# Sums turned on VectorE in 32x32 blocks, nine buffers for P, and last chunks tile by tile

## The chip, the cores and the metric

The kernel runs on one core of a Trainium2 chip. The metric is the time of one execution on the device in microseconds (us), the median of several runs. The engines are TensorE (PE; its weight loads are listed apart as PEld), VectorE (DVE), ScalarE (ACT), GpSimd (POOL) and SyncE (SP). DMAs are issued by SP and, at a few places, by ACT; an instruction that issues one occupies its engine's queue for as long as the issue takes, and everything behind it there waits.

## The reference

The program computes attention and two feed-forward layers behind it, all in float32 (weights of the first layer arrive as 64-bit floats):

```python
q_rot, k_rot = rotate(q), rotate(k)                    # 4 batches, 8 heads, 576 positions, 64 wide
scores = matmul(q_rot, k_rot.T) / 8
attn = exp(scores - max(scores))
attn = attn / (sum(attn) + 1e-9)
x = matmul(attn, v)                                    # -> 2304 tokens x 512
h = maximum(x @ w_in, 0);  x2 = (h * h) @ w_out        # 512 -> 2048 -> 512
h = x2 @ w_in2;  g = maximum(h, 0) + alpha * minimum(h, 0)
out = g @ w_out2                                       # 512 -> 2048 -> 512
```

## The kernel before, in words

**Attention** (function `attention`, from line 66) works on 16 pairs of heads: 4 batches by 4 pairs of neighbouring heads (`n` counts them, 0 to 15). For one pair the steps are: K and Q are rotated on GpSimd (`rope`), turned by TensorE (`turn`) and split into a high and a low part; scores are computed by query tile `i` (0 to 4, the fifth of 64 rows for both heads, called **S4**) and head `j` (`scores`, L257, three products per half for the split parts); VectorE takes the row maximum (`top`, L262, tile `nm`); ScalarE takes the exponential with its row sum (`exps`, L271), the sum into one of the columns of `sums`; TensorE turns P (`trans`, L279, `trans_tail`, `trans_end`); the results are copied out of PSUM (`leave`, tiles `pt`, `ptt`); TensorE multiplies with V (`pv`, L341) in two halves of 288 columns into a bank `acc`; and `store` copies each half to a tile `st` (L177 on ACT, L179 on DVE) and, with the second one, sends the tile to `x` in DRAM (L351).

P is not divided before it meets V. Instead the reciprocals of the sums travel apart: `over` (**OD**, L317 and L318) adds 1e-9 and takes the reciprocal on VectorE; `over_turn` (**O**, L322) turns the 128x32 tile of sums by a TensorE product with the identity; `over_leave` (**OR**) copies nine rows to a tile `ri` on ScalarE (L328) and stores them to a DRAM array `r` with three DMAs (L331 twice, L332). The queue for x and r is SP, for the last two pairs ACT.

**The order** of attention is written out by a plan. `PLAN` gives each step of a pair a due time within a repeating period, and the engine that takes a copy where there is a choice ("A" or "V"). All steps of all pairs lie in one heap and are recorded by due time, pair `n` at n periods plus the step's time, so each engine works on parts of three pairs at once. The due times set an order only; nothing waits for a clock. `NP_` is the number of buffers of a P tile; `acc` (`NAC`) and `st` have one buffer each.

**The first feed-forward layer** (function `moe`) works on 6 blocks of 384 tokens. For a block it loads x and r in four chunks of 128 columns: `load_x` (L764, L766, tile `xt`, two buffers) issues one DMA of x and two of r, broadcast over 64 rows each; `join_x` (L772, on GpSimd for these) multiplies them, and `high_x` and `low_x` split the product. Chunks of the first blocks are prepared while attention still runs: `AHEAD_X` steps from 13.5 pairs on, and the steps of `FOLLOW_AT` within the last pair's time, each call `follow`, which takes the next piece of the layer's start: chunk loads, joins, weight loads (L501, tile `w64`), the weights' conversion on VectorE and ScalarE (`convert` L510, L511; `mask` L516; `grow` L520; `sign` L525, L526; `join` L531, L532), and the first units of products (L803 to L805: 12 products of 384 columns make one unit). These products stand among attention's own in TensorE's order, so they fill TensorE between the last pairs' steps. Behind the last pair the layer runs alone.

**The second layer** has three groups of two blocks and forms its first product by seven block products. Its second product (L822) adds up 16 chunks of the hidden width, chunk after chunk, into three accumulators, one for each tile of 128 tokens; when chunk 15 is through, `finish` copies the accumulators out (L860 on ACT, L862 on DVE) and `store` sends the rows to `out` by SP (L834), in one or two DMAs per tile.

Of the kernel before, what the change touches and what calls it, by code (L numbers as in the profile page):

```python
# [23 lines left out]
P = 128  # L24
# [10 lines left out]
NP_, NTB, NAC = 8, 3, 1  # L35
PTB = 2
RB = 1
PERIOD = 14.053
PLAN = {
# [26 lines left out]
def attention(tc, q, k, v, ident_d, rope_d, xd, rd, follow):  # L66
# [10 lines left out]
    with ExitStack() as at:  # L77
# [237 lines left out]
        def over(n):  # L315
            t = sums[n][:, 0:9]
            V.tensor_scalar(t, t, 1e-9, None, ALU.add)  # L317
            V.reciprocal(t, t)  # L318

        def over_turn(n):  # L320
            u = turned[n, "o"] = bank()
            T.transpose(u[0:32, 0:P], sums[n], ident)  # L322
# [696 lines left out]
```

## Time and profile before

| | us |
|---|---|
| median of 3 runs | 1055.24 (1054.94 to 1055.89) |
| the profiled execution, whole | 1058.53 |
| its span, first to last instruction | 1056.7 |
| TensorE busy in it | 1040.0 |
| VectorE busy | 712.2 |
| ScalarE busy | 585.1 |
| GpSimd busy | 375.6 |

The profile shows one execution. Its own time is some 3.3 us above the median of the runs, so a sum made from its rows is a difference, to be set against its own time and carried over to the median. Times within it count from the span's start. Attention takes the first 280 us, the two layers the rest. A row such as "S4 ... [0.28 <-ACT p L271]" says that the engine sat idle for 0.28 us before this instruction, and that what it waited for last was ScalarE's instruction on tile `p` of line 271. Idle time of an engine that is not the bottleneck costs nothing by itself; here TensorE is busy nearly all the time, so the few places where it is idle are the ones to look at. "PEclk" is the clock that TensorE was granted, as a share of full speed.

### The profile page before, as it was taken

To read this page: it belongs to the slowest core of one execution; us is meant where nothing else is said; L and a number is where in the kernel's file an instruction comes from. 1 tells how busy PE (TensorE), PEld (TensorE's weight loads), DVE (VectorE), ACT (ScalarE), POOL (GpSimd) and SP (SyncE) were. 2 spreads that over 40 slices of the span, in tenths; PEclk is the share of its full clock that TensorE was granted. 3 is DMA by queue.
4 is the path that set the end of the run, shared out by engine and by line. 5 is a ranking of instruction groups with operands and counts; after the bars stand their busy time and mean duration, and the time that the engine had idled before them with its cause. 6 is when DMAs were issued, how large, how long until landed. Compare 5 with 4: busy or idle time off the path is not lost.

```text
span 1056.7 us, 20163 instructions
## 1 busy us (share of the span) xinstructions
PE 1040.0 (98%) x7512; PEld 925.2 (88%) x7512; DVE 712.2 (67%) x1263; ACT 585.1 (55%) x1281; POOL 375.6 (36%) x365
## 2 busy tenths in 40 slices
PE   9999999999999999999999999999999999999997
PEld 5777777776799999999999999999889998899886
DVE  5888878887699896897887876655354462644521
ACT  4788888886588454645546455344243442444321
POOL 6867566753000001423324133255212660146200
PEclk9999999999999999999999999999999999999999
DMA  7033223155254334556566557998015750177011
GB/s 192 2 92 92 68 83 91 47 157 165 86 160 138 120 97 137 191 189 232 182 209 221 175 192 279 327 307 253 8 60 185 254 181 14 47 235 250 25 30 30
DMA packets 101137, 153.23 MB, mean 145 GB/s; under 512 B 16944, under 2 KB 61360, under 8 KB 101040
## 3 DMA queue, kind: packets, MB, share of 16 engines
q1 hardware_dynamic: 100152, 150.81, 45.1%
q8 instruction: 59, 0.97, 0.4%
q10 hardware_dynamic: 888, 1.14, 0.3%
q14 instruction: 38, 0.31, 0.1%
HBM read 114.61 MB, written 37.30 MB: 144 GB/s over the span
## 4 chain that ended last, share of the span: by engine, by line
PE 89%; DVE 4%; DMA 3%; ACT 1%; POOL 1%; issue 1%; SPq 1%; ACTq 0%; POOLq 0%; DVEq 0%
PE py L822 26%; PE ph L714 17%; PE ph L822 9%; PE acc L341 6%; PE ph L803 6%; PE ph L804 6%; PE ph L805 6%; PE sc L257 6%; PE ps L279 4%; DMA xt<-r 2%; PE ps L198 1%; DVE nm L262 1%; DVE gl L755 1%; DMA w<-x 1%; ACT p L271 1%
## 5 line engine op out<-in xcount | busy, mean ns | idle before, releaser
L755 DVE TENSOR_TENSOR gl<-g,gh 128x384 fp32r<-128x384 f32 x189 | 130.5, 693 | 120.3 <-PE py L822 104.2
L748 ACT ACTIVATE gh<-g 128x384 fp32r<-128x384 f32 x189 | 98.1, 521 | 146.7 <-PE py L822 142.1
L714 PE MATMUL ph<-T,xs 128*128 128x384 f32 x1008 | 176.4, 335 | 0.0
L714 PEld LDWEIGHTS ph<-T,xs 128*128 128x128 f32 x1008 | 175.3, 188 | 0.8 <-ACT w L706 0.4
L822 PE MATMUL py<-gh,w 128*128 128x384 f32 x560 | 146.2, 335 | 0.0
L262 DVE TENSOR_REDUCE nm<-sc 128x1 f32<-128x576 f32 x144 | 107.5, 755 | 38.2 <-PE sc L257 36.8
L803 PE MATMUL ph<-xs,held 128*128 128x384 f32 x368 | 123.7, 336 | 0.0
L805 PE MATMUL ph<-xs,held 128*128 128x384 f32 x368 | 123.5, 336 | 0.0
L804 PE MATMUL ph<-xs,held 128*128 128x384 f32 x368 | 123.4, 335 | 0.0
L271 ACT ACTIVATE p<-sc,nm 128x576 f32<-128x576 f32 x144 | 105.8, 736 | 23.5 <-DVE nm L262 23.2
L257 PE MATMUL sc<-nat 64*128 64x288 f32 x768 | 113.4, 307 | 1.0 <-ACT p L271 0.5
L822 PE MATMUL py<-w,gh 128*128 128x512 f32 x336 | 103.5, 389 | 0.0
L822 PEld LDWEIGHTS py<-gh,w 128*128 128x128 f32 x560 | 101.9, 188 | 0.0
L257 PEld LDWEIGHTS sc<-nat 64*128 64x128 f32 x768 | 98.8, 187 | 2.8 <-ACT p L271 1.9
L822 PE MATMUL py<-gl,w 128*128 128x384 f32 x280 | 94.1, 336 | 2.3 <-DVE gl L755 2.3
L772 POOL TENSOR_TENSOR xt<-xt 128x384 f32<-128x384 f32 x24 | 26.5, 1108 | 192.4 <-DMA xt<-x 172.2
L702 POOL TENSOR_TENSOR g<-g,m 128x384 f32<-128x384 f32 x62 | 67.1, 1089 | 72.3 <-ACT g L701 72.3
L279 PE MATMUL ps<-ident,p 64*128 64x64 f32 x1152 | 87.4, 226 | 1.8 <-ACT pt L177 1.7
L279 PEld LDWEIGHTS ps<-ident,p 64*128 64x128 f32 x1152 | 78.1, 139 | 9.9 <-issue 7.4
L341 PE MATMUL acc<-pt,vraw 128*64 128x288 f32 x512 | 79.8, 423 | 1.7 <-ACT pt L177 1.3
L822 PEld LDWEIGHTS py<-w,gh 128*128 128x128 f32 x336 | 63.0, 188 | 13.0
L803 PEld LDWEIGHTS ph<-xs,held 128*128 128x128 f32 x368 | 69.4, 188 | 0.6 <-issue 0.4
(161 smaller groups left out, 2132.4 us busy)
## 6 DMA issues: line engine op xcount, KB each, us to landing
xs<-ws SPq DMA_DIRECT2D x168, 256.0 KB
w<-in_moe_w_in_dram SPq DMA_DIRECT2D x32, 512.0 KB
w<-in_moe_w_out_dram SPq DMA_DIRECT2D x32, 512.0 KB
ws<-w SPq DMA_DIRECT2D x40, 256.0 KB
wk<-xs SPq DMA_DIRECT2D x16, 512.0 KB
w<-wk SPq DMA_DIRECT2D x14, 512.0 KB
xt<-x SPq DMA_DIRECT2D x24, 192.0 KB
xt<-r SPq DMA_DIRECT2D x48, 96.0 KB
```

The lines of the kernel that those rows point to most:

```text
L257: T.matmul(t[:, x, 0:SH], lhsT=lhs, rhs=k[b][h, c0:c0 + SH], start=y == 0, stop=y == 2)
L262: V.tensor_reduce(out=nm[n, i, j], in_=sc[n, i, j][:, :, 0:SH], axis=AX.XY, op=ALU.max, negate=True)
L271: A.activation(out=Pt[n, i][:, j * S:(j + 1) * S].rearrange("p (a b) -> p a b", a=2), in_=sc.pop((n, i, j))[:, :, 0:SH], func=AF.Exp, bias ...
L279: T.transpose(u[:, 64 * k:64 * k + 64], Pt[n, i][halves[h], c0:c0 + P], ident[halves[h], halves[h]])
L341: T.matmul(acc[n, hf][64 * j:64 * j + 64, 0:SH], lhsT=v2[:, j, c], rhs=t, start=c == 0, stop=c == 4)
L714: T.matmul(bank[c], lhsT=w[:, y0, ws_], rhs=t[:, y1], start=first_ and kc == 0 and n == 0, stop=kc == 1 and n == 2, skip_group_check=not f ...
L748: A.activation(out=hi, in_=hidden(layer, b, i), func=AF.Copy)
L755: V.tensor_tensor(out=lo, in0=hidden(layer, b, i), in1=gsp[u][0].bitcast(F32), op=ALU.subtract)
L803: T.matmul(ph[:, :W], lhsT=wh[:, cs], rhs=xh, start=(c == 0), stop=False)
L804: T.matmul(ph[:, :W], lhsT=wh[:, cs], rhs=xl, start=False, stop=False)
L805: T.matmul(ph[:, :W], lhsT=wl[:, cs], rhs=xh, start=False, stop=(c == KC - 1))
L822: T.matmul(acc, lhsT=x, rhs=y, start=(s0 and k == 0), stop=(s1 and k == 2))
```

## The change

Four things change.

1. The turn of the sums goes from TensorE to VectorE. `over` calls a VectorE transpose, which turns each 32x32 block of the 128x32 tile by itself; the result `rows` has, in each group of 32 partitions, nine rows of 32 positions. `over_turn` and `over_leave` with their steps O and OR are gone. `store` sends the reciprocals, directly behind x and on the same queue, with five DMAs: four of eight rows by 32 positions (one for each group of 32 partitions), and one for the tail.
2. `PLAN` and `FOLLOW_AT` have new numbers (the period goes from 14.053 to 14.054; the last step is at 37.08, before at 40.01), and some copies change engine.
3. P has nine buffers instead of eight.
4. In the last block of the second layer, chunks 13 and 14 are held back until chunk 15; then each of the three accumulators takes its products of the three chunks in turn. The second DMA of the last tile goes out by ACT's queue.

```diff
-NP_, NTB, NAC = 8, 3, 1
+NP_, NTB, NAC = 9, 3, 1
...
-    "PV14": (38.512, ""), "O": (39.246, ""), "ST1": (39.257, "A"), "OR": (40.006, ""),
+    "PV14": (36.220, ""), "ST1": (37.084, "V"),
...
             V.reciprocal(t, t)
-
-        def over_turn(n):
-            u = turned[n, "o"] = bank()
-            T.transpose(u[0:32, 0:P], sums[n], ident)
-            yield
-
-        def over_leave(n):
-            b, hp = pairs[n]
-            r = sm.tile([9, P], F32, name="ri")
-            A.activation(out=r, in_=turned.pop((n, "o"))[0:9, 0:P], func=AF.Copy)
-            eng = nc.scalar if n + 2 >= pairs_n else nc.sync
-            for j in range(2):
-                eng.dma_start(out=rd[hp, j, b * S:b * S + 512].rearrange("(i p) -> i p", i=4), in_=r[4 * j:4 * j + 4, :])
-            eng.dma_start(out=rd[hp:hp + 1, :, b * S + 512:b * S + 576], in_=r[8:9, :].rearrange("o (j c) -> o j c", j=2))
+            rows[n] = sm.tile([P, 32], F32, name="rows", bufs=2)
+            V.transpose(rows[n], sums[n])
...
-                (nc.scalar if n + 2 >= pairs_n else nc.sync).dma_start(out=xd[:, hp, b * S:(b + 1) * S], in_=sts.pop(n))
+                eng = nc.scalar if n + 2 >= pairs_n else nc.sync
+                eng.dma_start(out=xd[:, hp, b * S:(b + 1) * S], in_=sts.pop(n))
+                r, t = rd[hp, :, b * S:(b + 1) * S], rows.pop(n)
+                for g in range(4):
+                    eng.dma_start(out=r[:, 0:512].rearrange("j (i g p) -> g j i p", i=4, g=4)[g], in_=t[32 * g:32 * g + 8])
+                eng.dma_start(out=r[:, 512:576].rearrange("j (c p) -> j c p", c=2), in_=t[8:P:32])
...
+            held_back.append((i, wh, wl, gh, gl))
+            if (layer, b) == (1, NB - 1) and FC - LAST <= i < FC - 1:
+                return
             for e, acc in enumerate(accs[layer, b]):
                 es = slice(e * P, (e + 1) * P)
+                for x, wh, wl, gh, gl in held_back:
...
+            held_back.clear()
...
-                nc.sync.dma_start(out=rows, in_=y[c - t * P:c - t * P + w, :])
+                (nc.scalar if t == NTT - 1 and c > t * P else nc.sync).dma_start(out=rows, in_=y[c - t * P:c - t * P + w, :])
```

How instructions stand is shown at three places. First TensorE in the steady attention, around the six products of S4 of one pair (`qt` holds the two heads' last query rows); before:

```order
L198 MATMUL ps_3044<-ident_79,rotq_2705 128x64 x2
L341 MATMUL acc_3005<-pt_2553,vraw1_120 64x288 x2
L341 MATMUL acc_3005<-ptt_2552,vraw1_120 64x288 x2
L322 MATMUL ps_3072<-ident_79,sums_135 32x128
L257 MATMUL sc_3076<-nat_2758,qt1_130 128x288 x6
L341 MATMUL acc_3098<-pt_2842,vraw0_117 64x288 x2
```

and the same place after:

```order
L222 MATMUL ps_2766<-ident_79,rotk_2246 128x64
L257 MATMUL sc_2749<-nat_2463 128x288
L329 MATMUL acc_2770<-pt_2540,vraw1_120 64x288 x4
L257 MATMUL sc_2778<-nat_2463,qt0_129 128x288 x6
L329 MATMUL acc_2770<-pt_2540,vraw1_120 64x288 x2
L279 MATMUL ps_2793<-ident_79,p_2632 128x64
```

The turn of the sums (L322) is gone from its place ahead of S4, and the products with V that end an `acc` no longer stand there.

Second SP's queue from the store of pair 12 to that of pair 13, with chunk loads (`xt`) in between; before:

```order
L351 DMA x1_63<-st_4454 128x576
L331 DMA r1_64<-ri_4583 4x128 x2
L332 DMA r1_64<-ri_4583 2x1x64
L764 DMA xt_4188<-x1_63 128x384
L766 DMA xt_4188<-r1_64 64x384 x2
L764 DMA xt_4188<-x1_63 128x384
L766 DMA xt_4188<-r1_64 64x384 x4
L764 DMA xt_4188<-x1_63 128x384
L766 DMA xt_4188<-r1_64 64x384 x2
L764 DMA xt_4188<-x1_63 128x384
L766 DMA xt_4188<-r1_64 64x384 x4
L351 DMA x1_63<-st_4753 128x576
```

and after, from the end of pair 12's store on:

```order
L343 DMA r1_64<-rows_4358 2x4x32 x4
L344 DMA r1_64<-rows_4358 2x2x32
L758 DMA xt_4167<-x1_63 128x384
L760 DMA xt_4167<-r1_64 64x384 x2
L758 DMA xt_4167<-x1_63 128x384
L760 DMA xt_4167<-r1_64 64x384 x2
L758 DMA xt_4167<-x1_63 128x384
L760 DMA xt_4167<-r1_64 64x384 x3
L758 DMA xt_4167<-x1_63 128x384
L760 DMA xt_4167<-r1_64 64x384 x3
L758 DMA xt_4167<-x1_63 128x384
L760 DMA xt_4167<-r1_64 64x384 x4
```

Behind the last row pair 13's x follows, as before (L340, `x1_63<-st_4684`). Ten chunk loads and the stores of pairs 10, 11 and 12 stand from the first chunk load to that store in both orders; each store has five DMAs of r instead of three.

Third TensorE where the first unit of the layer (`ph`, L803 to L805 before, L797 to L799 after) meets pair 14's products with V (`acc`, the first half and then the second); before:

```order
L805 MATMUL ph_4976<-xs_4180,held0_4864 128x384
L279 MATMUL ps_4971<-ident_79,p_4597 128x64 x2
L341 MATMUL acc_4852<-pt_4634,vraw1_120 64x288 x2
L341 MATMUL acc_4852<-ptt_4633,vraw1_120 64x288 x2
L279 MATMUL ps_4971<-ident_79,p_4597 128x64
L279 MATMUL ps_5005<-ident_79,p_4801 128x64 x8
L279 MATMUL ps_5017<-ident_79,p_4597 128x64 x4
L279 MATMUL ps_5024<-ident_79,p_4832 128x64 x8
L341 MATMUL acc_5034<-pt_4634,vraw1_120 64x288 x2
L803 MATMUL ph_5039<-xs_4180,held0_4864 128x384
```

and after:

```order
L329 MATMUL acc_4830<-pt_4628,vraw1_120 64x288 x2
L329 MATMUL acc_4830<-ptt_4627,vraw1_120 64x288 x2
L279 MATMUL ps_4925<-ident_79,p_4783 128x64 x8
L309 MATMUL ps_4937<-ident_79,p_4616 128x64
L279 MATMUL ps_4941<-ident_79,p_4649 128x64 x8
L329 MATMUL acc_4951<-pt_4628,vraw1_120 64x288 x4
L797 MATMUL ph_4960<-xs_4159,held0_4862 128x384
```

Before, one whole unit lies ahead of the end of the first half's `acc`, and the second unit behind the first products of the second half. After, no unit lies ahead of the second half's first products; three units lie among the attention work behind them (before, two), and then comes the layer's run without attention. On VectorE the copy of the first half to `st` stands ahead of the last step of the first weight block in the new order, behind it in the old one; on ScalarE the store of pair 14 (x and five DMAs of r) stands ahead of one copy of `pt` and of `grow` of the third weight block, and VectorE's further steps on that block and the converts of the next two stand ahead of the copy that frees `acc` for the last half.

## Rows read from the trace of the kernel before

**Rows 1.** The page: busy us, share of the span, instructions.

```profile
PE 1040.0 (98%) x7512; PEld 925.2 (88%) x7512; DVE 712.2 (67%) x1263; ACT 585.1 (55%) x1281; POOL 375.6 (36%) x365
```

**Rows 2.** Busy us of PE, PEld, DVE, ACT, POOL by stretch; clock, DMA.

```profile
110.00:150.00 40.00, 39.67 (x519) 28.42 (x515) 33.03 (x65) 33.70 (x87) 28.46 (x24) 1.00 0.26 76
249.00:270.00 21.00, 18.65 (x155) 13.47 (x157) 14.79 (x29) 9.38 (x20) 3.44 (x4) 0.92 0.48 157
281.00:320.00 39.00, 39.00 (x227) 39.00 (x226) 31.70 (x58) 33.12 (x63) 0.00 (x0) 1.00 0.43 130
```

**Rows 3.** The chain of waits, next pair's S4: start, us, what.

```profile
115.52 1.06 PE sc L257 x6
```

**Rows 4.** Timeline around S4: start, us, engine, line, operation, [idle <-releaser].

```profile
100.33 0.28 PE L322 MATMUL ps<-ident,sums 128*32 128x128 f32 x1
...
100.45 0.20 ACT L271 ACTIVATION_READ_ACCUMULATOR p<-sc,nm 128x1 f32 x1
...
100.70 0.82 PEld L257 LDWEIGHTS sc<-nat,qt 128*128 128x128 f32 x6 [0.28 <-ACT p L271]
```

**Rows 5.** Groups by line and shape: busy us, mean ns, idle before.

```profile
L318 DVE RECIPROCAL sums<-sums 128x9 f32<-128x9 f32 x16 | 3.4, 215 | 0.5
```

**Rows 6.** SP's queue: the first chunk load and pair 13's x.

```profile
215.98 0.35 SPq L764 DMA_DIRECT2D xt<-x  x1
...
255.73 0.53 SPq L351 DMA_DIRECT2D x<-st  x1
```

**Rows 7.** Issues of the old r stores: ns minimum, median, maximum.

```profile
L331 SPq DMA_DIRECT2D r<-ri x28: 247/282/327, 57.0 to 256.7; - x28
...
L332 SPq DMA_DIRECT2D r<-ri x14: 595/616/676, 57.6 to 257.0; - x14
```

**Rows 8.** The chain of waits in the drain: start, us, what.

```profile
243.94 3.81 DMA xt<-r
...
248.93 2.13 DMA xt<-r
...
261.20 1.35 PE acc L341 x8
...
270.74 0.38 PE ph L803
...
273.03 0.64 PE ps L279 x8
273.67 1.12 PE acc L341 x8
...
277.81 2.65 PE acc L341 x20
```

**Rows 9.** Timeline of the drain, TensorE and VectorE.

```profile
256.32 1.08 PE L279 MATMUL ps<-ident,p 64*128 64x64 f32 x17 [1.19 <-ACT pt L177]
...
262.63 0.46 DVE L179 COPY st<-acc 128x288 f32<-128x288 f32 x1 [3.47 <-PE acc L341]
...
280.43 0.42 PE L803 MATMUL ph<-xs,held 128*128 128x384 f32 x1
```

**Rows 10.** Timeline of the drain, ScalarE and VectorE.

```profile
269.81 0.35 ACTq L351 DMA_DIRECT2D x<-st  x1
...
273.71 0.60 ACT L177 ACTIVATE pt<-ps 128x512 f32<-128x512 f32 x1 [0.79 <-PE ps L279]
274.20 0.76 ACT L520 ACTIVATE w<-w,pbias 128x512 uint32<-128x512 uint32 x1
...
275.29 0.69 DVE L525 SCALAR_TENSOR_TENSOR w<-w 128x512 uint32<-128x512 uint32 x1
276.02 0.43 DVE L526 TENSOR_SCALAR w<-w 128x512 uint32<-128x512 uint32 x1
```

**Rows 11.** Timeline of the end: SP's issues, the last copy.

```profile
1050.37 3.68 SPq L834 DMA_DIRECT2D out_dram<-g  x6
...
1051.11 0.60 ACT L860 ACTIVATE g<-py 128x512 f32<-128x512 f32 x1 [0.76 <-PE py L822]
```

More of the change, by code (lines that the diff above doesn't have):

```diff
@@ L34 @@
 PAIRS = 16
-NP_, NTB, NAC = 8, 3, 1
+NP_, NTB, NAC = 9, 3, 1
 PTB = 2
 RB = 1
-PERIOD = 14.053
+PERIOD = 14.054
 PLAN = {
[16 rows of a table removed]
[16 rows of a table added]
 }
@@ L58 @@
 X_AT, X_EVERY = 13.5, .12
-FOLLOW_AT = (0, 12.38, 12.91, 14.33, 14.34, 15.59, 15.63, 17.51, 17.52, 17.68, 17.69, 19.61, 20.89, 20.9, 21.23, 24.16, 24.17, 25.21, 26.43, 26.44, 28.94, 29.68, 29.69, 31.73, 33.66, 39.87)
+FOLLOW_AT = (0, 12.99, 13.52, 14.48, 14.49, 16.11, 16.87, 18.59, 18.6, 18.98, 18.99, 20.29, 20.99, 22.14, 22.26, 24.45, 24.46, 24.47, 26.46, 29.83, 30.04, 30.92, 30.93, 32.64, 36.19, 36.93)
 ET = mybir.EngineType
@@ L187, in low @@
                 V.scalar_tensor_tensor(out=dst, in0=src, scalar=scale, in1=hi.bitcast(F32), op0=ALU.mult, op1=ALU.subtract)
-        sums, Pt, PT, sc, nm, sts, acc, turned = {}, {}, {}, {}, {}, {}, {}, {}
+        rows, sums, Pt, PT, sc, nm, sts, acc, turned = {}, {}, {}, {}, {}, {}, {}, {}, {}
         all_sums = st_.tile([P, 3, 32], F32, name="sums")
@@ L382, in attention @@
         products = {"S": (scores, 6, .125), "KQ": (turn, 8, .063), "X": (turn_tail, 1, 0), "T": (trans, 8, .063),
-                    "U": (trans_tail, 4, .063), "W": (trans_end, 1, 0), "O": (over_turn, 1, 0), "PV": (pv, 1, 0)}
+                    "U": (trans_tail, 4, .063), "W": (trans_end, 1, 0), "PV": (pv, 1, 0)}
         others = {"R": top, "E": exps, "C": leave, "CU": leave_tail, "CW": leave_end, "KH": turn_high, "KL": turn_low, "ST": store,
-                  "XQ": qtail_high, "QL": qtail_low, "XK": ktail_high, "XL": ktail_low, "OD": over, "OR": over_leave}
+                  "XQ": qtail_high, "QL": qtail_low, "XK": ktail_high, "XL": ktail_low, "OD": over}
         def queue(n, name):
@@ L466 @@
 HELD0, OUT0, OUTX, AHEAD = 4, 7, 2, 2
+LAST = 3
 FIRST_AT = -1, 0, 1, 2
@@ L812, in products @@
             gh, gl = gsp.pop(u)
-            s0, s1 = i == 0, i == FC - 1
+            held_back.append((i, wh, wl, gh, gl))
+            if (layer, b) == (1, NB - 1) and FC - LAST <= i < FC - 1:
+                return
             for e, acc in enumerate(accs[layer, b]):
                 es = slice(e * P, (e + 1) * P)
-                if layer == 0:
-                    acc = acc[:, :W]
-                    ops = [(x[:, es], y) for x, y in ((wh, gh), (wh, gl), (wl, gh))]
-                else:
-                    ops = [(x[:, es], y) for x, y in ((gh, wh), (gh, wl), (gl, wh))]
-                for k, (x, y) in enumerate(ops):
-                    T.matmul(acc, lhsT=x, rhs=y, start=(s0 and k == 0), stop=(s1 and k == 2))
+                for x, wh, wl, gh, gl in held_back:
+                    if layer == 0:
+                        acc = acc[:, :W]
+                        ops = [(l[:, es], r) for l, r in ((wh, gh), (wh, gl), (wl, gh))]
+                    else:
+                        ops = [(l[:, es], r) for l, r in ((gh, wh), (gh, wl), (gl, wh))]
+                    for k, (l, r) in enumerate(ops):
+                        T.matmul(acc, lhsT=l, rhs=r, start=(x == 0 and k == 0), stop=(x == FC - 1 and k == 2))
+            held_back.clear()
+        held_back = []
         def store(y, t):
```

30 rows, old and new, of the table PLAN are left out of this document.

## The prediction, made before the changed kernel was run

> **What bounds the kernel now.** I read the page's busy times first: TensorE works 1040.0 of 1056.7 us, 98% [rows 1]. So the time moves only where an edit takes TensorE work away or makes TensorE wait. The table by stretches says where it waits. In the steady attention (110 to 150 us) it is idle 0.33 of 40 us; in the drain of attention (249 to 270 us) 2.35 of 21; in the MoE run behind it (281 to 320 us) not at all [rows 2]. A delay of the MoE run's start is therefore paid to the end of the program. I take that start as the first product that has no attention work behind it, at 280.43 us [rows 9].
>
> **O off TensorE.** The diff removes one transpose of the sums and one copy `ri` per pair. O's matmul lies directly ahead of the six products S4 in the order shown; it begins at 100.33 us and S4 at 100.70, 0.37 us per pair [rows 4]. But S4 then waits 0.28 us for ScalarE, whose accumulator read of `p` ends at 100.45 + 0.20 = 100.65, O or not [rows 4]. S4 can follow sooner only by as much as that exponential itself comes sooner. The pair's period is 14.82 us (S4 again at 115.52 [rows 3]), and every engine but TensorE has slack in it, so part of O's time comes back. Bounds: 0 and 0.37 us a pair; I take the middle, 0.2. Against it stands the new block transpose on VectorE. The trace has none; the nearest row is the reciprocal of the same sums, 0.215 us for 9 of the 32 columns [rows 5]. I take 0.2, with half and twice the row, 0.1 and 0.43, as bounds. VectorE is busy 33.03 of 40 us [rows 2], so 0.2 us per 14.8 fits in its idle time. Where the cover is gone, the reduction behind it, for which the exponential waits, is late by that much, which is why I keep a pair at 0.2 and not 0.37. Up to the first X chunk, at 13.5 pairs, the gain is 13.5 × 0.2 = 2.7 us (bounds 0 and 5.0).
>
> **The stores' queue.** What blocks by 32 cost is DMAs: a pair stored x and three pieces of r; now it stores x and five pieces, all from SP behind x (ScalarE's queue for pairs 14 and 15). The new pieces are unseen. The nearest rows are the two old r forms: 4x128 takes 0.282 us to issue, the strided 2x1x64 takes 0.616 [rows 7]. The new ones have strided pieces of 128 bytes, so I take 0.6, the strided row, and keep 0.3 as the lower bound: per store 5 × 0.6 = 3.0 instead of 2 × 0.28 + 0.62 = 1.2 (1.25 with gaps), +1.75 us. The Trainium skill ("VectorE: DVE Perf Modes", The three transpose paths) states VectorE's transpose of a 128x128 bf16 tile as the faster one, 0.311 us against TensorE's 0.390, but in separate 32x32 blocks; going by those figures alone the swap would gain 0.08 us, and no row here shows them. While attention goes on, SP has idle time for that. Not in the X chain. From the first chunk's load at 215.98 us to pair 13's store at 255.73 SP goes through ten chunk loads of x and r, which wait for their two buffers and for POOL's join, and three stores, 39.75 us [rows 6]. The order of SP shows the same ten loads and three stores ahead of pair 13's store after the change. So the chain becomes 39.75 + 3 × 1.75 = 45.0 us. It starts 2.7 us earlier, at 213.3, and pair 13's x is issued at 258.3. From issue to landing the chain of waits shows 2.13 to 3.81 us for such transfers [rows 8]; with 2.9 x has landed at **261.2 us**. By the Trainium skill ("DMA: Bandwidth & Descriptors", Issuing engines are not separate DMA queues) the time a sequencer takes to issue is usually small beside the transfer. The strided row speaks against it here, as five of these come to more than one landing; by that rule the result would be the first rival.
>
> **Who waits for that landing.** `st` has one buffer, so the first `st` copy of pair 14 must wait for it, and `acc` has one too, so the second half's products of pair 14 wait for that copy. Before, this is hidden: VectorE waits at that copy for TensorE, 3.47 us until 262.63 [rows 9], because TensorE does its first MoE unit, from 256.32 + 1.08 = 257.40 on [rows 9], ahead of the last products of `acc`, which end at 261.20 + 1.35 = 262.55 [rows 8]. The new plan puts the unit behind the second half's first products. TensorE comes to them at about 262.55 − 3.8 (from 257.40 to 261.20, the unit and two transposes) − 2.7 (the gain) + 1.5 (17 transposes of the new order and the two, 0.64 per 8 [rows 8]) = 257.5 us, and waits until about 261.2 + 0.56 = 261.8: some 4 us with nothing to do. Behind that wait stand TensorE's first unit and, on VectorE, whose copy it is, the first two weight blocks' last steps.
>
> **From the copy to the MoE run.** In the new order, from the copy's start: copy 0.46 [rows 9] and release 0.1; 8 products 1.12, one unit 2.29 (270.74 to 273.03), 24 transposes 1.6, 8 products 1.12, a unit 2.29, 4 products 0.5 [rows 8]; copy of the second half 0.46. That is 9.9. Then ScalarE issues x (0.35) and five pieces (3.0), which stand ahead of a `pt` copy 0.60 and of the weight step `grow` 0.76 [rows 10]. VectorE's next rows wait for that; its passes over a weight block take 0.69 with two tensor operands and 0.43 with one [rows 10]: sign 0.69 + 0.43, ScalarE's `held` about 0.7, join 0.69, the next convert and mask 0.43 + 0.69 + 0.43, add, reciprocal and transpose 0.6, another convert 1.12, a 64x64 copy about 0.2, and then the copy that frees `acc` for the last half, 0.46 + 0.1. Last come that half's 20 products, 2.65 [rows 8]. Altogether 9.9 + 0.35 + 3.0 + 1.36 + 1.12 + 0.7 + 0.69 + 1.55 + 0.6 + 1.12 + 0.2 + 0.56 + 2.65 = 23.8 us; before, it is 280.43 − 262.63 = 17.8 [rows 9]. The MoE run starts at 261.2 + 23.8 = 285.0, **+4.6 us**.
>
> **The clock.** TensorE was idle 1.19 us before 256.32 [rows 9], and the granted clock of 249 to 270 us is 0.92, against 1.00 around it [rows 2]: a stretch at 1.2 GHz that costs up to 21 × 0.08 = 1.7 us. Two longer waits may bring one dip more, in or ahead of the MoE run. I take half, **+0.8** (bounds 0 and 1.7).
>
> **The end.** The last tile's accumulators now finish one after the other. Before, they finish together, and six output DMAs fill SP for 3.68 us from 1050.37 to 1054.05, though the last copy ends at 1051.11 + 0.60 = 1051.71 [rows 11]. Chunk by chunk the earlier tiles' DMAs are issued before that; the last tile's two go on two queues, so the last issue ends about 0.6 us behind the copy, at 1052.3: **−1.7** (bounds −1.2 and −2.5, from one issue more or none). The held-back products need `gh` and `gl` of the last chunk no sooner than 8 products behind before; VectorE is idle there.
>
> **Nine buffers for P** free an exponential from waiting for an old P; the views show no such wait, so nothing either way.
>
> **Sum.** +4.6 + 0.8 − 1.7 = +3.7 us. The profiled execution, 1058.53 us (span 1056.7 and 1.8 around it), is 3.3 above the median 1055.24; so 1062.2 for it and **1058.9, say 1059.0, for the median**. One term decides: the issue time of a piece counts 5 × 4 = 20 times (three stores in the chain, pair 14's), so 0.1 us of it is 2 us, and the sum is nil at 0.6 − 3.7/20 = 0.42 us.
>
> **Rivals.**
> (1) *Faster: the pieces issue at the plain row's 0.3 us.* Place: SP's queue between the chunk loads; it decides below 0.42. The chain then has 39.75 + 3 × 0.25 = 40.5 us, x has landed at 213.3 + 40.5 + 2.9 = 256.7; TensorE itself is ready at 257.5, so the wait there is all but gone, and 23.8 − 1.5 = 22.3 us follow the copy's start at 257.0: the MoE run starts near 279.3 (−1.1); no further dip, −1.7 at the end: **1052.4**. For it: the pieces are small and four of them alike. Against it: every strided r row is at 0.6 or more [rows 7].
> (2) *O's removal gives nothing,* because S4 waits for ScalarE, as it does now for 0.28 us [rows 4]. Then the chunk chain starts at 215.98 as before, x lands at 263.9, the MoE run starts at 287.7 (+7.3): +6.4, **1061.6**.
> (3) *No change:* the pieces near 0.42 us, or the chunk chain has gaps (each load waits for POOL) into which the longer stores fall, and gain and loss cancel: **1055.2**.
>
> **Chances.** The forecast 0.45; rival 2, 0.17; rival 3, 0.16; rival 1, 0.22. A measurement of this kernel tells some 0.2%, 2.1 us, from no change: slower 0.62, same 0.16, faster 0.22. Range: down, rival 1 with the tail's better bound, 1051.5; up, rival 2 with the full dip and a landing of 3.81 us, 1061.6 + 0.9 + 0.9 + 0.5 (tail), about 1064.0. The forecast's own range is 1057 to 1062.
>
> **What would show it.** In the new profile: S4 pieces about 14.6 us apart (0.2 less); the pieces' issue rows at 0.6 us; pair 13's x issued near 258; the first `st` copy of pair 14 waiting for a DMA, no longer for TensorE; TensorE idle some 4 us ahead of the second half of pair 14 and 5 ahead of pair 15's; the MoE run near 285; no six DMAs in a row at the end. Wrong would be: issue rows at 0.3, S4's distance unchanged, or an MoE run that starts by 281.

## The result, and the profile after

The changed kernel takes 1069.64 us (median of 4 runs, 1068.2 to 1070.71) where the kernel before takes 1055.57 beside it (1054.94 to 1058.94): a ratio of 1.0126, 95% interval 1.0101 to 1.0151. It is 14 us slower; slower by 3.8 was forecast, with 1064.0 as the end of the range. The span of the profiled execution is 1068.4 us, 11.7 more than before's.

The page of the changed kernel, busy times and then the shares of the chain that ended last, answers to [rows 1]:

```profile
PE 1044.4 (98%) x7464; PEld 924.6 (87%) x7464; DVE 722.0 (68%) x1295; ACT 570.9 (53%) x1249; POOL 379.1 (35%) x365
...
PE 82%; ACT 5%; DVE 5%; DMA 4%; SPq 1%; issue 1%; POOL 1%; ACTq 0%; DVEq 0%; POOLq 0%
```

TensorE is busy 4.4 us more with 48 instructions fewer, so its instructions were slowed, not multiplied; and a part of the chain has gone from TensorE to the other engines, ScalarE above all (before, TensorE held 89% and ScalarE 1%). The stretches (us, then busy time and count of PE, PEld, DVE, ACT and POOL, the granted clock, DMA share, GB/s) answer to [rows 2]:

```profile
110.00:150.00 40.00, 39.67 (x520) 28.18 (x517) 33.68 (x67) 31.18 (x81) 26.70 (x22) 1.00 0.24 73
...
249.00:270.00 21.00, 15.78 (x114) 10.95 (x113) 12.05 (x23) 7.93 (x18) 8.09 (x9) 0.70 0.46 138
...
281.00:300.00 19.00, 13.11 (x67) 9.57 (x66) 10.66 (x23) 5.23 (x10) 0.00 (x0) 0.82 0.23 71
```

In the drain of attention TensorE is idle for over 5 of 21 us and then for 6 of 19, and its clock is down to 0.70 and 0.82. The steady stretch looks as before by its busy time, and that is deceptive: S4's distance, which answers to [rows 3], has grown. Two neighbouring pairs' S4 in the timeline of TensorE:

```profile
101.44 1.06 PE L257 MATMUL sc<-nat,qt 128*128 128x288 f32 x6
...
116.60 0.66 PE L257 MATMUL sc<-nat,qt 128*128 128x288 f32 x3
```

That is 15.16 us a pair, where it was 14.82 and 14.6 was forecast. The last pair's S4 begins at 252.29 us (before 248.86), the run of MoE at 294.12 (before 280.43), the last product at 1063.71 (before 1050.68). So the 11.7 us of the span are made up of +3.4 up to the last S4, +10.3 from there to the run of MoE, −0.7 in that run and −1.3 behind the last product. Two of these terms flatter the change, because before's profiled execution lost time to the clock in the same places: it is at 0.92 from 249 to 270 us [rows 2] and once more in the run of MoE. The execution of e3 (below), which has the same attention and an undisturbed clock in both, needs 29.7 us from the last S4 to the run of MoE (before 31.6) and 768.3 for that run up to the last product (before 770.3). Against it the changed kernel loses 12.1 us in the drain and 1.3 in the run of MoE. The same stretch in both, first before, then e3:

```profile
380.00:420.00 40.00, 38.24 (x212) 37.88 (x211) 31.65 (x57) 19.21 (x39) 3.32 (x3) 0.96 0.38 122
```

```profile
380.00:420.00 40.00, 38.21 (x221) 37.86 (x220) 31.79 (x57) 19.15 (x37) 4.09 (x4) 1.00 0.46 146
```

The drain, in the timelines of VectorE, TensorE and ScalarE, answers to [rows 9] and [rows 10]:

```profile
255.56 0.46 PE L279 MATMUL ps<-ident,p 64*128 64x64 f32 x4 [0.42 <-ACT pt L177]
256.61 0.27 PE L309 MATMUL ps<-ident,p 64*128 64x64 f32 x1 [0.60 <-DVE pt L179]
...
264.72 0.46 DVE L179 COPY st<-acc 128x288 f32<-128x288 f32 x1 [4.58 <-DMA x<-st]
...
265.23 2.19 PE L329 MATMUL acc<-pt,vraw 128*64 128x288 f32 x8 [3.92 <-DVE st L179]
...
277.71 0.36 ACTq L340 DMA_DIRECT2D x<-st  x1
278.11 3.08 ACTq L343 DMA_DIRECT2D r<-rows  x4
281.23 0.50 ACTq L344 DMA_DIRECT2D r<-rows  x1
281.78 0.60 ACT L177 ACTIVATE pt<-ps 128x512 f32<-128x512 f32 x1 [7.18 <-DMA r<-rows]
...
289.13 4.11 PE L329 MATMUL acc<-pt,vraw 128*64 128x288 f32 x16 [5.89 <-DVE st L179]
...
294.12 0.69 PE L797 MATMUL ph<-xs,held 128*128 128x384 f32 x1
```

Both waits that were forecast are there: the first copy of pair 14 waits for the landing of pair 13's x, and TensorE 3.92 us behind it; then ScalarE's queue is closed by the issues of r, and TensorE waits 5.89 us for the copy ahead of the last half. What was not forecast is how slow TensorE is behind each wait: 8 products take 2.19 us (before 1.12), 16 take 4.11 (before 20 took 2.65 [rows 8]).

### The profile page after: what moved, and what is told of

Read it like the earlier page. It is cut to its first block, busy times and chain, and to the rows that moved or that the text cites. A ratio compares the mean times of both kernels' runs of the same rounds, so it can differ in the third digit from the quotient of the medians.

```text
span 1068.4 us, 20040 instructions
## 1 busy us (share of the span) xinstructions
PE 1044.4 (98%) x7464; PEld 924.6 (87%) x7464; DVE 722.0 (68%) x1295; ACT 570.9 (53%) x1249; POOL 379.1 (35%) x365
## 4 chain that ended last, share of the span: by engine, by line
PE 82%; ACT 5%; DVE 5%; DMA 4%; SPq 1%; issue 1%; POOL 1%; ACTq 0%; DVEq 0%; POOLq 0%
PE py L819 26%; PE ph L708 16%; PE ph L819 8%; PE ph L797 6%; PE ph L798 6%; PE ph L799 6%; PE sc L257 5%; PE acc L329 3%; PE ps L279 3%; ACT p L271 2%; DMA kraw<-in_k_dram 1%; DVE nm L262 1%; ACT nat L177 1%; DMA xt<-r 1%; ACT pt L177 1%
## 5 line engine op out<-in xcount | busy, mean ns | idle before, releaser
L797 PE MATMUL ph<-xs,held 128*128 128x384 f32 x368 | 124.4, 338 | 0.0
L799 PE MATMUL ph<-xs,held 128*128 128x384 f32 x368 | 123.5, 336 | 0.0
L257 PE MATMUL sc<-nat 64*128 64x288 f32 x768 | 110.0, 311 | 0.6 <-ACT nat L177 0.4
L257 PEld LDWEIGHTS sc<-nat 64*128 64x128 f32 x768 | 89.9, 186 | 12.1 <-ACT p L271 10.2
L329 PE MATMUL acc<-pt,vraw 128*64 128x288 f32 x512 | 82.4, 435 | 9.8 <-DVE st L179 9.8
L279 PE MATMUL ps<-ident,p 64*128 64x64 f32 x1152 | 81.4, 230 | 1.0 <-ACT pt L177 1.0
L279 PEld LDWEIGHTS ps<-ident,p 64*128 64x128 f32 x1152 | 67.2, 140 | 16.0 <-issue 13.4
L514 ACT ACTIVATE w<-w,pbias 128x512 uint32<-128x512 uint32 x64 | 48.8, 763 | 53.6 <-DVE w L510 44.6
```

The costliest lines, as they stand in the source:

```text
L257: T.matmul(t[:, x, 0:SH], lhsT=lhs, rhs=k[b][h, c0:c0 + SH], start=y == 0, stop=y == 2)
L279: T.transpose(u[:, 64 * k:64 * k + 64], Pt[n, i][halves[h], c0:c0 + P], ident[halves[h], halves[h]])
L329: T.matmul(acc[n, hf][64 * j:64 * j + 64, 0:SH], lhsT=v2[:, j, c], rhs=t, start=c == 0, stop=c == 4)
L797: T.matmul(ph[:, :W], lhsT=wh[:, cs], rhs=xh, start=(c == 0), stop=False)
L799: T.matmul(ph[:, :W], lhsT=wl[:, cs], rhs=xh, start=False, stop=(c == KC - 1))
```

## The experiments

Two questions were put first: whether the new plan or the turn on VectorE makes the pairs come later, and what the waits of the drain are worth. Each run of the kernel before stands beside the runs it is compared with. Its median moved between 1055.18 and 1057.46 us from one group of runs to the next, so a difference between two changed kernels of different groups is known to some 2 us only.

**e1: the turn on VectorE with the old plan.**

```diff
-NP_, NTB, NAC = 9, 3, 1
+NP_, NTB, NAC = 8, 3, 1
-PERIOD = 14.054
+PERIOD = 14.053
...
-    "PV14": (36.220, ""), "ST1": (37.084, "V"),
+    "PV14": (38.512, ""), "ST1": (39.257, "A"),
...
-            if (layer, b) == (1, NB - 1) and FC - LAST <= i < FC - 1:
+            if (layer, b) == (1, NB - 1) and False:
```

> The plan, FOLLOW_AT and eight P buffers of before, without O and OR; the sums are turned by VectorE and stored by five DMAs behind x as in the change; nothing of the end is changed. Theory A (the new plan makes the steady attention longer, by its order and its sides): S4 comes every 14.6 to 14.82 us as I had reckoned for the turn alone, and only the stores' extra issue time (5 x 0.57 instead of 1.25 us) is paid in the drain: the time lies between -2 and +3 us of before, 1053 to 1059. Theory B (the block transpose stands ahead of reductions on VectorE and delays the exponentials): S4 comes every 15.1 us here too and the time is 1062 or more.

Measured: 1063.28 us against 1055.18, ratio 1.0073 (1.0048 to 1.0099). S4 stays at 14.82 us, in the timeline of TensorE:

```profile
101.04 1.06 PE L257 MATMUL sc<-nat,qt 128*128 128x288 f32 x6 [0.30 <-ACT p L271]
...
115.86 0.40 PE L257 MATMUL sc<-nat,qt 128*128 128x288 f32 x1 [0.31 <-ACT p L271]
```

Theory B falls: the block transpose does not lengthen the pair on this plan. But my own term falls with it: O is gone and S4 comes not a bit sooner. The groups by line between 75 and 205 us (busy us, mean ns, then idle time ahead of them) show where O's 0.37 us went, weight loads of S4, first of before, then of e1:

```profile
L257 PEld LDWEIGHTS sc<-nat,qt 128*128 128x128 f32 x53 | 7.3, 188 | 2.5 <-ACT p L271 2.5
```

```profile
L257 PEld LDWEIGHTS sc<-nat,qt 128*128 128x128 f32 x50 | 6.9, 188 | 7.3 <-ACT p L271 7.3
```

Over some nine pairs (six loads each) S4 waits for ScalarE's exponential 0.28 us a pair with O ahead of it and 0.88 without. O stood in a wait. That theory A's time came out too high (1053 to 1059 expected) has another cause, which the trace names: from 215 to 250 us the block transpose itself waits for the DMAs of r from two pairs before, since `rows` has two buffers.

```profile
227.50 0.21 DVE L320 STREAM_TRANSPOSE rows<-sums 128x32 f32<-128x32 f32 x1 [1.77 <-DMA r<-rows]
...
245.47 0.21 DVE L320 STREAM_TRANSPOSE rows<-sums 128x32 f32<-128x32 f32 x1 [3.24 <-DMA r<-rows]
```

The reductions stand behind it, and TensorE waits 2.89 us for an exponential at 247.39. In the old plan `over` has its place at 16.97 and the store at 39.26; the new plan puts `over` at 29.99, which makes this wait go.

**e2: the new plan with the turn on TensorE.**

```diff
-    "PV14": (36.220, ""), "ST1": (37.084, "V"),
+    "PV14": (36.220, ""), "O": (36.3, ""), "ST1": (37.084, "V"), "OR": (37.2, ""),
...
-            rows[n] = sm.tile([P, 32], F32, name="rows", bufs=2)
-            V.transpose(rows[n], sums[n])
+
+        def over_turn(n):
+            u = turned[n, "o"] = bank()
+            T.transpose(u[0:32, 0:P], sums[n], ident)
+            yield
...
```

> The changed kernel, but the sums are turned by TensorE (a step O ahead of ST1, OR behind it) and stored by the three old DMAs. Theory A: S4 still comes about every 15.16 us or later (O costs 0.3 us of TensorE again), and only the drain gains, some 3 to 6 us of issue time: 1064 to 1070. Theory B: S4 comes every 14.8 us and the time falls to 1060 or less.

Measured: 1071.36 against 1055.18, ratio 1.0142 (1.0122 to 1.0161). Theory A holds: S4 comes every 15.37 us, in the timeline of TensorE:

```profile
102.61 1.06 PE L257 MATMUL sc<-nat,qt 128*128 128x288 f32 x6
...
117.98 1.06 PE L257 MATMUL sc<-nat,qt 128*128 128x288 f32 x6
```

Against 15.16 with the turn on VectorE that is the 0.2 us a pair that I had forecast for O, on the new plan; against 14.82 with the same turn on the old plan, the new plan costs 0.55 us a pair. The drain does gain what was expected of it, 35.9 us from the last S4 (255.95) to the run of MoE instead of 41.8, but the pairs have lost 3.7 us of that by then. In its profile the run of MoE then takes 2.2 us longer than in the changed kernel (771.8 for 769.6), which was not traced. The three old DMAs also show what the longer stores cost in SP's chain: 221.74 to 261.95 us from the first chunk load to pair 13's x, 40.2 us, where the changed kernel takes 42.25.

**e3: the end alone,** put into the kernel before (`LAST`, `held_back`, the second DMA of the last tile on ACT).

```diff
+            held_back.append((i, wh, wl, gh, gl))
+            if (layer, b) == (1, NB - 1) and FC - LAST <= i < FC - 1:
+                return
...
-                nc.sync.dma_start(out=rows, in_=y[c - t * P:c - t * P + w, :])
+                (nc.scalar if t == NTT - 1 and c > t * P else nc.sync).dma_start(out=rows, in_=y[c - t * P:c - t * P + w, :])
```

> The kernel before with the change of the end alone (last chunks tile by tile, the last tile's second DMA on ACT's queue). My prediction's term: -1.7 us (-1.2 to -2.5), 1053.5; the rival, that issue on two queues saves nothing because the data go through the same DMA engines: -1.2 us or less. The two profiles' ends differ by 1.2 us after the last product.

Measured: 1055.35 against 1055.18, ratio 0.9997 (0.9985 to 1.0009): not to be told from before. By the profiles the last product begins 4.7 us ahead of the end of the span (1047.01 of 1051.7), before 6.0 (1050.68 of 1056.7), so 1.3 us are saved behind the last product, which lies within the interval. The end of the changed kernel, timelines of SP and ACT, answers to [rows 11] (its last product begins at 1063.71 us):

```profile
1060.68 4.54 SPq L834 DMA_DIRECT2D out_dram<-g  x5
...
1064.13 0.60 ACT L860 ACTIVATE g<-py 128x512 f32<-128x512 f32 x1 [3.48 <-PE py L819]
1064.76 0.57 ACTq L834 DMA_DIRECT2D out_dram<-g  x1
```

Five issues now spread over 4.5 us beside the products, and the sixth goes out on ACT as soon as the last copy is done.

**e4: two buffers for `st`** in the changed kernel.

```diff
-                sts[n] = sm.tile([P, S], F32, name="st", bufs=1)
+                sts[n] = sm.tile([P, S], F32, name="st", bufs=2)
```

> The changed kernel with two buffers for st instead of one, so that the first copy of pair 14 does not wait for the landing of pair 13's x. If that landing is what TensorE waits for at 261 to 265 us, the wait of 3.9 us goes, the clock does not fall behind it, and the time is 4 to 7 us under the changed kernel's, 1063 to 1066. The rival (VectorE's and ScalarE's queues hold the drain by themselves): under 2 us.

Measured: 1064.14 against 1055.18, ratio 1.0075 (1.0054 to 1.0097), 5.5 us under the changed kernel's 1069.64 (5.1 if each is set against the before beside it). The wait of 3.92 us is gone, and the 8 products behind it take 1.19 us instead of 2.19; the wait ahead of the last half stays, 5.90 us. The landing is what TensorE waited for. The clock still falls ahead of that place (0.76 from 255 to 262 us) and is then back at 1.00 from 262 to 270; in the changed kernel it stays low until nearly 271. So the wait did not start the slow stretch, but without it the stretch is shorter.

**e5 and e6: order against sides.** The new plan also moves eleven copies to another engine. e5 has the new due times with the old sides, e6 the kernel before with the new sides.

These are XK, XQ1, C10, C41, C31, C30, CU1, CU0, C21, CW0 and ST1; one of them in each kernel:

```diff
-    "PV14": (36.220, ""), "ST1": (37.084, "V"),
+    "PV14": (36.220, ""), "ST1": (37.084, "A"),
```

```diff
-    "PV14": (38.512, ""), "O": (39.246, ""), "ST1": (39.257, "A"), "OR": (40.006, ""),
+    "PV14": (38.512, ""), "O": (39.246, ""), "ST1": (39.257, "V"), "OR": (40.006, ""),
```

> The changed kernel with the old plan's choice of engine for the eleven copies whose side the change moved; the new due times stay. S4 came every 15.16 us in the changed kernel and every 14.82 before. Theory A1 (the sides: VectorE has got 0.7 us more per pair ahead of its reductions): S4 comes every 14.9 us or less and the time is 4 us or more under the changed kernel's 1069.6. Theory A2 (the order: scores and turns of P stand in blocks and score tiles wait for their exponentials): S4 stays at 15.1 us or more, the time at 1068 or more.

> The kernel before with the new plan's engine for those eleven copies; due times, turn by TensorE and stores of before. Theory A1: S4 comes every 15.0 us or more, time 1059 or more. Theory A2: S4 stays near 14.82 us and the time within 2 us of before.

Measured: e5 1074.11 against 1057.12, ratio 1.0168 (1.0143 to 1.0193), S4 every 15.30 us; e6 1098.25, ratio 1.0388 (1.0368 to 1.0407), S4 every 17.8 us. TensorE in one pair of e6, matmuls of S4 and those that waited:

```profile
147.71 1.05 PE L255 MATMUL sc<-nat,qt 128*128 128x288 f32 x6
149.87 0.27 PE L277 MATMUL ps<-ident,p 64*128 64x64 f32 x1 [0.26 <-DVE nat L183]
151.56 0.27 PE L277 MATMUL ps<-ident,p 64*128 64x64 f32 x1 [0.71 <-ACT ptt L175]
155.68 0.40 PE L255 MATMUL sc<-nat 64*128 64x288 f32 x1 [0.39 <-ACT p L269]
162.53 0.40 PE L255 MATMUL sc<-nat 64*128 64x288 f32 x1 [0.45 <-ACT p L269]
165.49 0.80 PE L255 MATMUL sc<-nat,qt 128*128 128x288 f32 x4
```

In e6 the products of TensorE wait four times a pair for copies and exponentials, 1.8 us together; the pair is 2.9 us longer, so this is not the whole of it. The new order is slow with either choice of sides, and the sides are no free choice: each order needs its own. Moving the copies back is no cure; the order it is, but why was still open.

**e7: three buffers for `rows`** on e1.

```diff
-            rows[n] = sm.tile([P, 32], F32, name="rows", bufs=2)
+            rows[n] = sm.tile([P, 32], F32, name="rows", bufs=3)
```

> As e1 (plan of before, turn by VectorE) with three buffers of rows instead of two. In e1 the block transpose waited 5.0 us for the DMAs of r of two pairs before, in the stretch of the chunk loads, and TensorE lost 2.9 us there. If that wait is what e1 pays, it goes: S4 of the last pair comes 4 us sooner than e1's 253.7 and the time is 1057 to 1060; if not (the longer stores in SP's queue hold the rest), it stays within 1.5 us of e1's 1063.3. The steady distance of S4 stays 14.82 either way.

Measured: 1061.83 against 1057.12, ratio 1.0052 (1.0033 to 1.0071). The last S4 comes at 249.57, 4.2 us sooner than in e1, as expected, but the time missed its range (it is 1.5 us under e1's, 3.4 if each is set against the before beside it): TensorE now waits 1.69 us at 258.70 for a copy, and the run of MoE starts at 282.8 us, only 0.8 sooner than e1's 283.6. Most of the gain was given back in the drain, a part of it to the clock of this execution: it is 0.94 from 250 to 281 us, where e1's is 1.00.

**e8: r of the last two pairs issued by SP,** and **e9: this and the two buffers for `st`,** both on the changed kernel.

```diff
-                r, t = rd[hp, :, b * S:(b + 1) * S], rows.pop(n)
+                r, t, eng = rd[hp, :, b * S:(b + 1) * S], rows.pop(n), nc.sync
```

> The changed kernel, with the ten DMAs of r of pairs 14 and 15 issued by SP; x of these pairs stays with ScalarE. ScalarE then goes from x's issue straight to the copy of pt and to grow. By my working this takes 3.0 us off the path from the first copy of pair 14 to the run of MoE: TensorE's wait of 5.9 us at 283 to 289 falls to about 3 and the time to 1066. The rival: the wait is set by VectorE's weight steps and the fall is under 1 us.

> The changed kernel with both edits of the drain: two buffers for st (alone -5.5 us) and r of pairs 14 and 15 issued by SP (alone -6.1 us). If the two waits of TensorE (3.9 us at pair 14's second half, 5.9 at pair 15's) are separate, the gains add up: about 1058 us. If they share a cause (the slow clock behind each, or the weights' steps), the time stays near 1061. S4 stays at 15.15 us, and the last one at 252.3, 3.4 us behind before: without that the drain's loss would be nearly gone.

Measured: e8 1063.53 against 1057.12, ratio 1.0065 (1.0049 to 1.0082), 6.1 us under the changed kernel (7.7 if each is set against the before beside it). TensorE at the last half, in e8:

```profile
285.40 2.16 PE L329 MATMUL acc<-pt,vraw 128*64 128x288 f32 x16 [2.22 <-DVE st L179]
```

The wait fell by 3.7 us, as long as the issues were, and with a wait of 2.22 us instead of 5.89 the 16 products behind it take 2.16 us instead of 4.11; the granted clock is 1.00 from 280 to 290 us. So the expected 3.0 us came with 1.9 of clock. e9 takes 1059.68 against 1056.69, ratio 1.0028 (1.0015 to 1.0041): the two gains nearly add up (11.6 by themselves, 10.0 together; 12.8 and 11.1 against the before beside each). With the first wait gone and the second cut to 2.22 us, the changed kernel is 3 us behind before, and 3.4 of lag it has already at the last S4 of the changed kernel.

**e10 and e13: reductions made short.** The row maximum is taken over 64 of the 576 columns, in e10 on the changed kernel, in e13 on the kernel before.

```diff
-            V.tensor_reduce(out=nm[n, i, j], in_=sc[n, i, j][:, :, 0:SH], axis=AX.XY, op=ALU.max, negate=True)
+            V.tensor_reduce(out=nm[n, i, j], in_=sc[n, i, j][:, :, 0:32], axis=AX.XY, op=ALU.max, negate=True)
```

> The changed kernel with the row maximum taken over 64 of the 576 columns only, so that VectorE's reductions are some 0.5 us shorter each (about 5 us of 15 per pair); the maximum is not the true one. Theory L (latency: in the new order score tiles wait for the reduction and the exponential behind it, held up on VectorE): S4 comes every 14.8 us or less. Theory P (TensorE itself: scores and turns stand in blocks of their own in the new order, and that costs it 0.55 us a pair however early the exponentials come): S4 stays at 15.1 us.

> The kernel before with the row maximum over 64 of the 576 columns, as e10 has it on the changed kernel. e10 brought S4 from 15.15 to 14.22 us. If the loop of score, reduction and exponential holds the steady attention in both orders, S4 falls here too, by 0.4 us or more from 14.82. If TensorE itself is the bound in the old order and the loop only in the new one, S4 stays within 0.15 us of 14.82 here.

Measured, one run each: 1057.53 us for e10 beside 1056.69, and 1051.43 for e13 beside 1057.46; S4 every 14.22 us in e10 and every 14.46 in e13. First e10's two rows, then e13's:

```profile
96.49 1.06 PE L257 MATMUL sc<-nat,qt 128*128 128x288 f32 x6
...
110.72 0.53 PE L257 MATMUL sc<-nat,qt 128*128 128x288 f32 x2
```

```profile
98.06 1.06 PE L257 MATMUL sc<-nat,qt 128*128 128x288 f32 x6
...
112.52 0.66 PE L257 MATMUL sc<-nat,qt 128*128 128x288 f32 x3
```

A reduction falls from 0.75 to 0.22 us. The new order gains 0.94 us a pair by that, the old one 0.36. e10 fits theory L; e13's 0.36 falls just short of the 0.4 set for it, but is well over the 0.15 of the other reading. So the length of the reductions is what holds the steady attention, in the new order far more than in the old, and TensorE's own work is no more than 14.22 us a pair in the new order and 14.46 in the old, O included. By which way the reductions hold it is not shown: it can be the loop from a score tile to its reduction, its exponential and back to the next scores in the same bank, as theory L has it, or the copies that stand behind the reductions in VectorE's queue and come sooner too. With the reductions short the new order is in front, 14.22 against 14.46; that gap is about the 0.2 that O's removal was to bring. The groups by line of the changed kernel between 75 and 205 us show who waits, exponentials, reductions and loads of scores:

```profile
L271 ACT ACTIVATE p<-sc,nm 128x576 f32<-128x576 f32 x78 | 57.4, 739 | 20.0 <-DVE nm L262 19.7
L262 DVE TENSOR_REDUCE nm<-sc 128x1 f32<-128x576 f32 x78 | 57.1, 751 | 10.6 <-PE sc L257 9.0
L257 PEld LDWEIGHTS sc<-nat 64*128 64x128 f32 x412 | 48.2, 186 | 6.4 <-ACT p L271 6.0
...
L257 PEld LDWEIGHTS sc<-nat,qt 128*128 128x128 f32 x48 | 6.6, 188 | 4.6 <-ACT p L271 4.6
```

and the same groups of the kernel before, without the reductions:

```profile
L271 ACT ACTIVATE p<-sc,nm 128x576 f32<-128x576 f32 x80 | 58.7, 735 | 7.8 <-DVE nm L262 7.8
...
L257 PEld LDWEIGHTS sc<-nat 64*128 64x128 f32 x420 | 54.6, 188 | 0.0
```

Over some nine pairs exponentials wait for a maximum 19.7 us instead of 7.8, and weight loads of scores wait for an exponential 6.0 + 4.6 = 10.6 instead of 2.5 (all of it at S4, as shown with e1). The first of the two goes with the pairs' distance, the second does not measure it. The same groups of e10:

```profile
L271 ACT ACTIVATE p<-sc,nm 128x576 f32<-128x576 f32 x82 | 60.1, 737 | 5.4 <-DVE nm L262 5.2
L257 PEld LDWEIGHTS sc<-nat 64*128 64x128 f32 x444 | 47.0, 186 | 4.7 <-ACT p L271 3.9
...
L257 PEld LDWEIGHTS sc<-nat,qt 128*128 128x128 f32 x54 | 7.4, 188 | 5.1 <-ACT p L271 5.1
```

There the exponentials' wait is down to 5.2, but the weight loads still wait 3.9 + 5.1 = 9.0 with pairs 0.94 us shorter; and in e1 they wait 7.3 with pairs as long as before's. The busy time of TensorE shows nothing of all this: its matmuls are pipelined and their ends are modelled, so a short wait can pass for work.

**e11: the kernel before with the new end and r of pairs 14 and 15 by SP.**

```diff
-            eng = nc.scalar if n + 2 >= pairs_n else nc.sync
+            eng = nc.sync
             for j in range(2):
                 eng.dma_start(out=rd[hp, j, b * S:b * S + 512].rearrange("(i p) -> i p", i=4), in_=r[4 * j:4 * j + 4, :])
```

> The kernel before with the change of the end (1.3 us sooner in the profile of e3) and r of pairs 14 and 15 issued by SP instead of ScalarE, which there take 1.5 us per pair of ScalarE's queue. If ScalarE's queue holds the drain of before as well, TensorE's wait of 1.11 us ahead of the last half shrinks: 1053.5 or less, the fastest of all. If it does not, as e3: within 1 us of before.

Measured: 1054.73 against 1056.69 (10 and 20 runs), ratio 0.9980 (0.9971 to 0.9989): 2 us in front of before, the fastest of the kernels that take the true maximum. But the wait it was aimed at is as it was, 1.12 us ahead of the last half at 276.25 (e3: 1.11 at 276.13), so the issues of r in ScalarE's queue did not set it. The end accounts for 1.3 of the 2 us; whether r by SP brings the rest, or the interval is just wide enough, stays open.

**e12: the old plan with all of it,** e7 with the new end and r of pairs 14 and 15 by SP.

```diff
-            rows[n] = sm.tile([P, 32], F32, name="rows", bufs=2)
+            rows[n] = sm.tile([P, 32], F32, name="rows", bufs=3)
-                r, t = rd[hp, :, b * S:(b + 1) * S], rows.pop(n)
+                r, t, eng = rd[hp, :, b * S:(b + 1) * S], rows.pop(n), nc.sync
...
-    "PV14": (36.220, ""), "ST1": (37.084, "V"),
+    "PV14": (38.512, ""), "ST1": (39.257, "A"),
```

> The plan of before with the turn by VectorE, three buffers of rows, the change of the end and r of pairs 14 and 15 issued by SP: the change without its new plan and with the waits taken away that the runs have found. e7 without the last two was 4.7 us behind before. Expected -1.3 for the end and -2 for the queue: about 1.5 us behind before, 1058. If the turn by VectorE were worth something on this plan, it would be in front of before.

Measured: 1060.25 against 1056.69, ratio 1.0035 (1.0017 to 1.0052), slower than expected. S4 comes every 14.82 us: the turn by VectorE is worth nothing on this plan. In its profiled execution the run of MoE starts at 283.2, 2.8 us behind before, and lasts 4 us longer; between 300 and 720 us TensorE waits 5.9 us in it instead of 2.8. What in the order makes these waits was not traced, and this execution, at 1064.11 us, was the slowest of the five, so the others need not have all of it.

**e14: eight buffers for P** in the changed kernel.

```diff
-NP_, NTB, NAC = 9, 3, 1
+NP_, NTB, NAC = 8, 3, 1
```

> The changed kernel with eight buffers for P. I had taken the ninth buffer at nothing. If the new plan keeps P longer so that it needs the ninth, an exponential waits for the turns of an older P, S4 comes later than every 15.16 us and the time is 1072 or more; if not, S4 stays at 15.16 and the time within 2 us of the changed kernel's 1069.6.

Measured: 1068.98 us, ratio 1.0110 (1.0084 to 1.0136) to before's 1057.46 beside it; S4 every 15.07 to 15.11 us. The ninth buffer is worth nothing here that can be told from zero.

## Why the prediction was right or wrong

Right: that it is slower, where the time goes in the drain, and most prices. The block transpose takes 0.212 us (0.2 was taken), and the stores of r by blocks cost what the strided row said, not the plain one [rows 7], by line: minimum, median and maximum ns:

```profile
L343 SPq DMA_DIRECT2D r<-rows x56: 567/576/727, 53.6 to 264.3; - x56
```

```profile
L344 SPq DMA_DIRECT2D r<-rows x14: 489/490/498, 56.3 to 264.9; - x14
```

Four at 0.576 and one at 0.49 are 2.8 us, forecast 3.0. With that rival 1 was out. By the Trainium skill ("DMA: Bandwidth & Descriptors", Issuing engines are not separate DMA queues) the time a sequencer takes to issue is usually small beside the transfer. Here one piece of r took 0.58 us to issue and the five of a store 2.8, beside 3.0 from the issue of x to the copy that its landing frees; together they were not small, and moving ten issues off ScalarE was worth 6.1 us (e8). From pair 13's x issue at 261.70 to the copy it frees at 264.72 it is 3.0 us (2.9); TensorE's wait there 3.92 (some 4), the second one 5.89 (5). That the first wait came out so close is in part luck: x landed 3.5 us later than forecast, and TensorE was ready 3.8 later, at 261.31 for 257.5. A late start of MoE is paid in full: that run takes 0.7 us less than before's and 1.3 more than e3's. The ninth buffer is worth nothing. By the profiles the end saves 1.3 us (1.7, bounds 1.2 to 2.5); the runs of e3 do not tell it from nothing.

Wrong, by size:

- **"S4 can follow sooner only by as much as that exponential itself comes sooner ... I take the middle, 0.2."** This is the step that failed. Half of the argument was right (S4 waits for ScalarE, O or not), and e1 shows that it was the whole of it on the old plan: 14.82 us. I then costed the turn alone and gave the new due times no price at all, though they move every score, reduction and exponential. They cost 0.55 us a pair (e2), of which O gives back 0.2. In the traces exponentials wait longer for VectorE's reductions in the new order, and with the reductions short the pair falls by 0.94 us there and by 0.36 in the old one (e10, e13); which step behind the reductions hands the delay on to TensorE stays open. Instead of −2.7 us up to the first chunk load (213.3) there were +3.5 (219.45), a miss of 6.1 us at the start of SP's chain. Rival 2 was the right mechanism on the wrong kernel: it had S4 at 14.82, and even that would have been too fast.
- **The chain of chunk loads: 45.0 us.** It took 42.25, from 219.45 to 261.70. Each store has grown by the issue time forecast, but by e2's 40.2 us the three stores lengthened the chain by 2.0, not 5.25: the rest would have fallen into gaps in which the chunk loads wait for transfers and GpSimd anyway, as rival 3 had it (that the gaps took it was not tried by itself). By luck, this made good nearly half of the first miss: pair 13's x was issued 3.4 us later than forecast, at 261.70 for 258.3.
- **The clock: +0.8.** Around the two waits the granted clock is at 1.2 GHz:

```profile
258.00:266.00 8.00, 3.80 (x25) 2.56 (x23) 3.27 (x9) 1.82 (x4) 1.00 (x1) 0.50 0.32 108
266.00:272.00 6.00, 6.00 (x36) 4.59 (x33) 1.83 (x4) 0.77 (x2) 0.00 (x0) 0.59 0.85 262
289.00:296.00 7.00, 6.87 (x29) 4.36 (x30) 4.14 (x8) 1.55 (x3) 0.00 (x0) 0.59 0.32 99
```

  As an estimate, busy time times the missing share, 3.80 × 0.50 + 6.00 × 0.41 + 6.87 × 0.41, is 7.2 us, where before lost 1.7 in its drain: +5.5. I had allowed for one more dip at half its price. From the copy at 264.72 to the run of MoE it is 29.4 us, forecast 23.8; 1.1 of the 5.6 us more is in the 8 products behind the first wait, 1.6 in the unit behind them (3.9 for 2.29 us), 2.3 in the last 20 (5.0 for 2.65).

In sum: pair 13's x 3.4 us later than forecast, 0.1 in the landing, 5.6 behind the copy, are the 9.1 us between 285.0 and 294.1; the separate +0.8 for the clock goes off, and −1.3 and −0.7 at the end stand against −1.7. That gives a span of 1068.4 where 1060.4 would have been the forecast's. Against the medians the miss is larger, 10.6 us, because the profiled execution of before was itself 3 us above its median (its two stretches of low clock, told with the result, account for most of that), while that of the changed kernel, 1070.16, was at its own.

## What to carry to other kernels

When a plan of order is exchanged, cost the new order by itself: follow one tile through the engines that hand it on (here scores, reduction, exponential) in the old order and in the new, since a table of due times can cost more than the operation whose removal it was made for. An operation ahead of an instruction that waits for another engine can be free: on the old plan the removal of O only made that wait longer (e1), on the new plan it brought 0.2 us a pair (e2). Issues of DMAs in a queue that also computes are worth moving to a queue that only issues, if a copy behind them is waited for: here ten of them cost 6 us, a third of it in slowed products behind the wait; on the kernel before, the same move left the wait as it was (e11).

## What the runs showed of the hardware

TensorE's granted clock was at 0.50, which is 1.2 GHz, from 258 to 266 us. TensorE had waited 0.42 and 0.60 us shortly ahead of that; the wait of 3.92 us began only at 261.3, when the clock was down already. Waits of 0.53 and 1.00 us at the same place of e1 were followed by no such stretch (1.00 from 250 to 281 us), so these runs do not tell what brings it on. A wait of 5.89 us was followed by 16 products in 4.11 us; the same products after a wait of 2.22 us took 2.16 (e8). So this wait cost a third of itself again, in the products behind it. And the busy time that the profile gives TensorE did not show a loss of 0.34 us a pair (39.67 of 40 us in both kernels). The idle time of the weight loads of scores is no measure of it either (2.5 us over nine pairs in the kernel before, 7.3 in e1 with pairs of the same length); the distance from one S4 to the next is.
